# Attention and a wave MLP on one core: q and k of two batches on all 128 partitions, a last key chunk of 128, the last residual by DMA, another order of the steps

## The chip, the core and the metric

The kernel runs on one core of a Trainium2 chip. The core has a matrix engine (PE, with its weight loads listed apart as PEld), three engines for elementwise work (DVE, ACT, POOL) and SP, whose queue issues nearly all DMAs here. Data come from the chip's memory through 16 DMA engines into SBUF, which has 128 partitions; PE writes to PSUM, which has eight banks. The metric is the device time of one execution in microseconds.

## The reference

The inputs are q, k, v of 8 batches, 8 heads, 576 tokens and 64 numbers a head. Two attentions are added, one on tokens averaged in fours, one on a band of three neighbours to each side, and the sum goes through a wave MLP:

```
q_d, k_d, v_d = means of 4 tokens of q, k, v                 # 144 tokens
out_up    = repeat(softmax(q_d k_d^T / 8) v_d, 4 times)      # pooled part
out_local = softmax(q k^T / 8 where |i - j| < 4) v           # band
x     = out_up + out_local, heads side by side               # 8 x 576 x 512
theta = x @ w_theta
y     = w_tok_r @ (x * cos(theta)) + w_tok_i @ (x * sin(theta))   # over tokens
u     = x + y
out   = u + max(u @ w_ch, 0)                                  # float32
```

## The kernel before

Each batch goes through a chain of generator functions; each `next` of one is a step. A string of letters says in which order the steps are taken, and `pin` ties the instructions of every engine to that order, so each engine's queue is in the order of the string. The letters, with the names that the text uses (batch behind the point):

- L `load`, C `cast`: q, k, v from memory in float32 into one of 8 staging buffers, then to bf16. For batches 0 and 1 (`WIDE`) a piece is two heads of q or k, six tokens on each of 96 partitions: pieces q0 to q3 and k0 to k3. From batch 2 on a piece is 2 x 96 tokens of all heads. v has five chunks of keys in three pieces. Casts run on DVE (q), ACT (k) and POOL (v) for batch 0 and on POOL for all others.
- A `turns`: PE turns q and k so that the head's numbers lie on partitions, and pools the tokens. Aq0 to Aq3 and Ak0 to Ak3 in the wide form (`wide_turn`: matmuls into a two-bank buffer, copied by ACT for q, by DVE for k, then DVE sums fours: qdT, kdP), 12 narrower steps else. Avd pools v; POOL multiplies it by `own`.
- S `scores`: Sd0 and Sd1 are the pooled scores, S0 to S4 those of the five chunks of the band; ACT takes exp. Outside the band DVE multiplies by a mask (batch 0), or POOL applies two selects (the others).
- N `pooled_out`: Ng0, Ng1 the pooled output, divided on DVE (xd), Nx its transposes. V `outputs`: V0 to V4 the band's output, divided on DVE (tmp).
- T `transposes`: x transposed, the pooled part added by DVE. H `phases`: theta on PE, sin and cos on ACT (cs). M, Z: x times cos and sin (z).
- X `mix`: X00 to X31, four channel blocks in two halves, 9 matmuls of 288 columns each into psu; DVE adds x (uT). The largest part of the work.
- U `residuals`: for the batches in `DMA_U`, 1 to 6, four DMA transposes of uT into `u_tm`. R `channels`: u @ w_ch into psr. Without the DMA, PE also transposes u (psx) and ACT takes the maximum (rel). O `store`: DVE adds, SP stores.
- l, c, W: the weights' loads (th0, th1, then r, i with their last 64 rows apart, ch), casts, and the nine transposed blocks of the token weights (WT, all needed by X). D: five groups of six warm-up matmuls (wu) on zeros, whose result nobody reads.

Two-bank PSUM buffers (`w2`) come in two copies, one-bank buffers (`w1`) in four; a step that takes a buffer waits until the step that held it has been copied out. The string has a first part, a period of 84 letters that is repeated three times (it takes one batch through every stage), and a last part. X00.0 is the first of the 64 X steps. Around the start the order is

```
Lq0 Lk0 Lq1 Cq0 Ck0 Lk1 Cq1 Aq0 Lq2 Lk2 Ak0 Lq3 Lk3 Ck1 Cq2 Aq1 Lv0 Ak1 Ck2 D0 Lv1 Cq3 Lv2 Aq2 D1 Ak2 Ck3 Aq3 lth0 Ak3 ...
```

all of batch 0, and later `... S3.0 cth0 D2 V0.0 ... Nx.0 V1.0 cr0 S4.0 D3 ... W0 ... T0.0 ... T1.0 ... V2.0 V3.0 H0.0`.

Of the kernel before, what the change touches and what calls it, by code (L numbers as in the profile page):

```python
# [15 lines left out]
P = 128  # L16
B = 8
# [12 lines left out]
KS = [0, 116, 236, 356, 476]  # L30
KW = [128, 128, 128, 128, 100]
# [5 lines left out]
NTR = 6  # L37
TP = TR // 4
# [9 lines left out]
def kernel(  # L48
# [34 lines left out]
    def stage(b, key):  # L83
        t = staged[b, key] = stg.tile([P, 1024], FP32, tag="st", name=f"st{b}_{key}")
        return t

    def load(b):

        if b < WIDE:
            for hh in range(4):  # L90
                for nm, src in zip("qk", (q, k)):
                    nc.sync.dma_start(
                        out=stage(b, f"{nm}{hh}")[0:TR, 0:2 * NTR * D].rearrange("p (h e) -> p h e", h=2),
                        in_=src[b, 2 * hh:2 * hh + 2].rearrange("h (p r) d -> p h (r d)", r=NTR),
                    )
                    yield
        else:
            for nm, src in zip("qk", (q, k)):
                for i in range(3):
                    t = stage(b, f"{nm}{i}")[0:TR].rearrange("p (c h d) -> p c h d", c=2, d=D)  # L100
                    for j in range(2):
                        c = 2 * i + j
                        nc.sync.dma_start(
                            out=t[:, j], in_=src[b, :, TR * c:TR * c + TR, :].rearrange("h p d -> p h d"),
                        )
                    yield
        for i in range(3):
            t = stage(b, f"v{i}").rearrange("p (c h d) -> p c h d", c=2, d=D)
            for c in range(2 * i, min(2 * i + 2, NCH)):
                nc.sync.dma_start(  # L110
                    out=t[0:KW[c], c % 2],
                    in_=v[b, :, KS[c]:KS[c] + KW[c], :].rearrange("h p d -> p h d"),
                )
            yield

    def cast(b):

        q_tm = work.tile([TR, NTR, H, D], BF16, tag="q_tm", bufs=1, name=f"q_tm{b}")
        k_tm = work.tile([TR, NTR, H, D], BF16, tag="k_tm", bufs=1, name=f"k_tm{b}")
# [3 lines left out]
        if b < WIDE:  # L123
            for hh in range(4):
                for i, dst in enumerate((q_tm, k_tm)):
                    eng[i](out=dst[:, :, 2 * hh:2 * hh + 2, :].rearrange("p r h d -> p h r d"),
                           in_=staged.pop((b, f"{'qk'[i]}{hh}"))[0:TR, 0:2 * NTR * D].rearrange(
                               "p (h r d) -> p h r d", h=2, d=D))
# [59 lines left out]
    for lo in (0, 4):  # L188
# [17 lines left out]
    for off in (3, -1):  # L206
# [39 lines left out]
    def weight_casts():  # L246

        for i in range(2):
            act(out=wth[:, 2 * i:2 * i + 2, :].rearrange("p c e -> p (c e)"), in_=staged.pop(("w", f"th{i}")))
# [7 lines left out]
        for i in range(2):  # L257
            gp(out=wch[:, 2 * i:2 * i + 2, :].rearrange("p c e -> p (c e)"), in_=staged.pop(("w", f"ch{i}")))
# [33 lines left out]
    def turns(b):  # L292
# [8 lines left out]
        def wide_turn(n, hh):  # L301
            tm, To = ((q_tm, qT), (k_tm, kT))[n]
            ps = w2(f"pstr{n}{hh}_{b}")
            for r in range(NTR):
                nc.tensor.matmul(
                    out=ps[:, r // 3, (r % 3) * TR:(r % 3) * TR + TR],
                    lhsT=tm[:, r, 2 * hh:2 * hh + 2, :], rhs=ip[:, 0:TR], start=True, stop=True,
                )
            (dve if n == 1 else act)(
                out=To[:, hh, :].rearrange("p (w k c) -> p w k c", k=2, c=3),  # L310
                in_=ps[:, :, 0:3 * TR].rearrange("p k (c w) -> p w k c", w=TR),
# [13 lines left out]
        def turn(n, c):  # L325
            tm, To = ((q_tm, qT), (k_tm, kT))[n]
            ps = w1(f"pstr{n}{c}_{b}")[:, 0:4 * TW].rearrange("p (hh w) -> p hh w", w=TW)
            for hh in range(4):
                nc.tensor.matmul(  # L329
                    out=ps[:, hh, :], lhsT=tm[:, c, 2 * hh:2 * hh + 2, :], rhs=ip, start=True, stop=True,  # L330
# [24 lines left out]
        for c in range(4):  # L355
            nc.tensor.matmul(out=psb[KP * c:KP * c + KP, 0:2 * D], lhsT=PU[1][0:KW[4], :],
# [15 lines left out]
    def scores(b):  # L372
# [43 lines left out]
        for c in range(NCH):  # L416
# [200 lines left out]
    def residuals(b):  # L617

        u = u_tm[b] = moep.tile([P, 4, 4, P], BF16, tag="utm", bufs=1, name=f"utm_{b}")
        for dc in range(4):  # L620
            nc.sync.dma_start_transpose(out=u[:, dc], in_=uTs[b][:, dc, 0:512])
# [45 lines left out]
    def store(b):  # L667
# [20 lines left out]
    DMA_U = (1, 2, 3, 4, 5, 6)  # L688
# [7 lines left out]
        "LLLCCLCALLALLCCALACDLCLADACAlAlCSSSClCSLASlScDVlNCcNAlNlVcSDlLcccWcTCLTcVVLHTAZCLVCHTCWALWWWLLTLLCCA"  # L696
        "LCWZWAAHLLAHWHADLWCSLCCCMZCLLZASlZlLCXSXACANSAACXLCSLNAAAXNSSXVAccCAXTCALVAACVLXLSTTSSHLVVXLTLHCTZRO"
        "AHZZCLHVLROHRLLMCOCSZZCNRLROSLNALOA"
    )
    PERIOD = (  # L700
        "XSCSNTXCCAAXCUAAVAXUACVAXAVAAVXTSSTAXSTAUTHXULCNHZNCAHLZCVHHCZROLLSLMSZRLOZRORLOLROL"
# [3 lines left out]
        "ASXVAAAXAAVXACCNAVXAUTACCCSUTTXTASSCXAHXVZUNHCTHXCAUHZNHZSZLLLRCMOLARORSSCZLRSOOCCNAXAXACAVAAVXXAVTA"  # L705
        "XUSSTARVXSOSXASTTHVUXVTHUNHZUZHNZHRMOSSZRORZORVXSONXTVTXXTVHXVXUHTZXTZHZUUHXZHMURROZROOXXRORXOXXXXRO"
        "ROXRORORORO"
# [61 lines left out]
```

## Time and profile before

| what | value |
|---|---|
| median of 13 runs | 261.26 us (259.7 to 262.89) |
| the profiled execution: time, span | 261.91 us, 260.2 us |
| PE busy (share of the span) | 242.9 us (93%) |
| DVE, ACT, POOL busy | 188.8 (73%), 178.8 (69%), 153.8 (59%) us |
| psu matmuls (L608), 576 of them | 80.0 us busy |
| warm-up matmuls (L282), 30 of them | 12.1 us busy |
| mean granted PE clock | 0.974 |
| DMA moved | 46.73 MB, 180 GB/s on the mean |

Busy times of PE overlap, since its matmuls are pipelined, so that a busy share does not say how many matmuls went through; the counts and the granted clock beside it do. The chain is followed back from the last instruction to what released each step. In the first 40 us PE's count in each 10 us is 26, 60, 85 and 95; from 40 to 50 it is 123.

### The profile page before, as it was taken

How to read it: one execution, taken by the hardware profiler on the slowest of the kernel's cores; microseconds unless marked ns; L12 is line 12 of the kernel's file. 1: busy time of each engine (PE TensorE's matmuls, PEld its weight loads, DVE VectorE, ACT ScalarE, POOL GpSimd, SP SyncE). 2: the span in 40 equal slices, each digit the busy share in tenths (PEclk: the TensorE clock that was granted, in tenths of full speed). 3: DMA queues.
4: the chain of work that ended last, by engine and by line, in shares of the span. 5: the costliest groups of instructions: out<-in, count | busy, mean ns of one | idle time of the engine just before them, and what ended most of it. 6: DMA issues, size and time to landing. Idle time of an engine off the chain costs nothing.

```text
span 260.2 us, 7472 instructions
## 1 busy us (share of the span) xinstructions
PE 242.9 (93%) x2960; PEld 170.1 (65%) x2960; DVE 188.8 (73%) x421; ACT 178.8 (69%) x336; POOL 153.8 (59%) x178
## 2 busy tenths in 40 slices
PE   1769699999999999999999999999999999999993
PEld 1325456678657876588667866687668666776762
DVE  4865869956777787868696868785777588876443
ACT  4349379997889778956896779777886787334022
POOL 4244345579997978398648956797169762600000
PEclk9995679999999999999999999999999999999999
DMA  7999999999999992899689997899399032311324
GB/s 197 231 239 323 260 242 194 214 219 233 220 219 236 237 169 52 195 217 268 126 170 221 279 156 142 177 254 226 58 242 248 23 63 81 105 40 43 142 73 152
DMA packets 120851, 46.73 MB, mean 180 GB/s; under 512 B 110448, under 2 KB 114544, under 8 KB 120816
## 3 DMA queue, kind: packets, MB, share of 16 engines
q1 hardware_dynamic: 120736, 46.18, 80.0%
q8 instruction: 23, 0.38, 0.7%
q14 instruction: 12, 0.10, 0.1%
q10 hardware_dynamic: 80, 0.07, 0.1%
HBM read 33.65 MB, written 9.44 MB: 166 GB/s over the span
## 4 chain that ended last, share of the span: by engine, by line
PE 85%; ACT 5%; DVE 5%; DMA 2%; issue 1%; SPq 0%; DVEq 0%
PE psu L608 27%; PE psr L632 11%; PE psth L546 10%; PE pstr L329 6%; PE psS L421 4%; PE psloc L498 4%; PE wu L282 3%; PE psxt L581 3%; PE xTps L528 3%; DMA st_k<-in_k_dram 2%; PE psnd L460 2%; PE psr L650 2%; PE pstl L557 1%; ACT pm L429 1%; PE psnd L466 1%; PE psxd L483 1%
## 5 line engine op out<-in xcount | busy, mean ns | idle before, releaser
L608 PE MATMUL psu<-WT,z 128*128 128x288 bf16 x576 | 80.0, 286 | 0.0
L608 PEld LDWEIGHTS <-z 128*128 128x128 bf16 x576 | 53.6, 98 | 15.2 <-issue 0.8
L442 POOL TENSOR_SCALAR_AFFINE_SELECT pm<-pm 128x1024 bf16<-128x1024 bf16 (+1 forms) x35 | 36.7, 1047 | 22.2 <-ACT pm L429 22.1
L612 DVE TENSOR_TENSOR uT<-psu,xT 128x288 bf16<-128x288 f32 x64 | 29.2, 456 | 24.2 <-PE psu L608 23.2
L429 ACT ACTIVATE pm<-psS 128x1024 bf16<-128x1024 f32 (+1 forms) x40 | 38.1, 984 | 10.7 <-PE psS L421 10.5
L444 POOL TENSOR_SCALAR_AFFINE_SELECT pm<-pm 128x1024 bf16<-128x1024 bf16 (+1 forms) x35 | 36.7, 1049 | 2.4
L546 PE MATMUL psth<-wth,xT 128*128 128x512 bf16 x128 | 32.9, 379 | 0.4 <-DVE xT L529 0.4
L632 PE MATMUL psr<-wch,uT 128*128 128x512 bf16 x128 | 32.0, 380 | 0.0
L551 ACT ACTIVATE cs<-psth,pihc 128x512 bf16<-128x512 f32 x32 | 22.0, 688 | 11.8 <-PE psth L546 8.0
L529 DVE TENSOR_TENSOR xT<-xTps,xdT 128x480 bf16<-128x480 bf16 (+1 forms) x40 | 24.9, 632 | 5.8 <-PE xTps L528 5.2
L507 DVE TENSOR_TENSOR tmp<-psloc,rl 120x512 bf16<-120x512 f32 (+1 forms) x40 | 27.6, 691 | 1.4
L139 POOL CAST v_w<-st_v 128x1024 bf16<-128x1024 f32 (+1 forms) x24 | 20.8, 896 | 10.6 <-DMA st_v<-in_v_dram 10.6
L582 DVE TENSOR_TENSOR z<-psxt,cs 128x1024 bf16<-128x1024 bf16 x32 | 21.7, 686 | 4.7 <-PE psxt L581 3.1
L133 POOL CAST k_tm<-st_k 96x1024 bf16<-96x1024 f32 x18 | 18.8, 1045 | 9.4 <-DMA st_k<-in_k_dram 8.4
L332 ACT CAST kT<-pstr 128x384 bf16<-128x384 f32 x36 | 18.0, 500 | 7.0 <-PE pstr L329 6.9
L662 ACT ACTIVATE rel<-psr 128x512 f32<-128x512 f32 (+1 forms) x16 | 7.9, 492 | 18.4 <-PE psr L650 15.0
L133 POOL CAST q_tm<-st_q 96x1024 bf16<-96x1024 f32 x18 | 18.4, 1035 | 2.4 <-DMA st_q<-in_q_dram 2.4
L332 ACT CAST qT<-pstr 128x384 bf16<-128x384 f32 x36 | 16.0, 481 | 4.9 <-PE pstr L329 4.7
L552 ACT ACTIVATE cs<-psth 128x512 bf16<-128x512 f32 x32 | 18.9, 590 | 0.0
L673 DVE SCALAR_TENSOR_TENSOR osb<-psr,utm 128x512 f32<-128x512 f32 x24 | 16.3, 687 | 2.3 <-PE psr L632 1.8
L632 PEld LDWEIGHTS <-uT 128*128 128x128 bf16 x128 | 11.1, 98 | 9.8
L498 PE MATMUL psloc<-v_w,pm 128*128 128x65 bf16 (+1 forms) x320 | 17.3, 197 | 0.0
(107 smaller groups left out, 439.1 us busy)
## 6 DMA issues: line engine op xcount, KB each, us to landing
st_v<-in_v_dram SPq DMA_DIRECT2D x32, 256.0 KB, 4.9
out_dram<-osb SPq DMA_DIRECT2D x32, 256.0 KB, 3.6
st_q<-in_q_dram SPq DMA_DIRECT2D x36, 192.0 KB, 4.9
st_k<-in_k_dram SPq DMA_DIRECT2D x36, 192.0 KB, 4.4
st_q<-in_q_dram SPq DMA_DIRECT2D x8, 288.0 KB, 6.1
st_k<-in_k_dram SPq DMA_DIRECT2D x8, 288.0 KB, 12.1
st_v<-in_v_dram SPq DMA_DIRECT2D x8, 200.0 KB
w<-in_moe_w_tok_r_dram SPq DMA_DIRECT2D x2, 576.0 KB
```

The source lines that it names most:

```text
L133: eng[i](out=dst[:, 2 * c:2 * c + 2].rearrange("p c h d -> p (c h d)"), in_=staged.pop((b, f"{'qk'[i]}{c}"))[0:TR])
L332: nc.scalar.copy(out=To[:, :, TR * c:TR * c + TR], in_=ps[:, :, 0:TR])
L429: nc.scalar.activation(out=pv, in_=ps[0:kw].rearrange("p e (j w) -> p (e j) w", w=P)[:, :, 0:qn], func=AF.Exp, scale=SCL,)
L442: nc.gpsimd.affine_select(out=pv, in_=pv, compare_op=ALU.is_ge, fill=0.0, base=off, pattern=[[0, 8], [-1, qn]], channel_multiplier=1)
L444: nc.gpsimd.affine_select(out=pv, in_=pv, compare_op=ALU.is_ge, fill=0.0, base=6 - off, pattern=[[0, 8], [1, qn]], channel_multiplier=-1)
L498: nc.tensor.matmul(out=pv[0:qn, par, j, :], lhsT=pms[b][c][0:kw, 4 * par + j, 0:qn], rhs=v_w[0:kw, c, 2 * j + par, 0:65], start=(j == 0), ...
L507: nc.vector.tensor_tensor(out=tmp[0:cnt].rearrange("p (j e d) -> p e j d", e=2, j=4), in0=pv[0:cnt, :, :, 0:D], in1=rl[0:cnt].unsqueeze(3) ...
L529: nc.vector.tensor_tensor(out=xT[:, :, QS[c]:QS[c] + cnt].rearrange("p e (m j) -> p e m j", j=4), in0=ps[:, :, 0:cnt].rearrange("p e (m j) ...
L546: nc.tensor.matmul(out=th, lhsT=xT[:, dc, P * c:P * c + P], rhs=wth[:, dc, :], start=(dc == 0), stop=(dc == 3),)
L608: nc.tensor.matmul(out=ps[:, 0:288], lhsT=z[:, j, P * dc:P * dc + P], rhs=WT[:, j, cols], start=(j == 0), stop=(j == 8),)
L612: nc.vector.tensor_tensor(out=uT[:, dc, cols], in0=ps[:, 0:288], in1=xT[:, dc, cols], op=ALU.add)
L632: nc.tensor.matmul(out=psr, lhsT=uT[:, dc, P * c:P * c + P], rhs=wch[:, dc, :], start=(dc == 0), stop=(dc == 3),)
```

## The change

- q and k of batches 0 and 1: a piece is now four heads (q0, q1, k0, k1). Heads 4g and 4g + 1 lie on partitions 0 to 63, the next two on 64 to 127, nine tokens of two heads on each partition; each half is a DMA of its own of 288 KB, so there are again 16 such DMAs for the two batches. Two casts for q and two for k take the place of four and four. A turn step has nine matmuls of 64 columns, with half of the identity as the moving operand, where it had six of 96.
- The last chunk of keys has 128 rows (448 to 575) in place of 100. A third pooling matrix (`PU[2]`) and a third mask (`band[2]`) are made for it.
- The last batch joins `DMA_U`: three of its four residual blocks are transposed by DMA, the fourth by PE with a copy on ACT. The maximum and the add of its four large pieces become one DVE instruction each.
- The string of steps is a new one in all three parts; the period is again 84 letters. At the start it now reads (batch 0 where none is given)

```
Lq0 Cq0 Lk0 Aq0 Ck0 Ak0 Lq1 Cq1 Aq1 D0 Ak1 Lk1 Ck1 lth0 Lv0 Aq2 Lv1 Lv2 cth0 Ak2 Cv0 Cv1 Cv2 Aq3 lth1 Ak3 Sd0 lr0 Sd1 lr1 S0 Avd S1 S2 lrt D1 cth1 V0 S3 cr0 cr1 li0 Ng0 li1 crt ci0 Ng1 lit Lq0.1 Lk0.1 Lq1.1 D2 ci1 Lk1.1 cit V1 Cq0.1 Nx V2 W0 T0 ... W1 T1 S4 V3 W2 Cq1.1 W3 ... T2 Lq0.2 Aq0.1 H0 V4 D3 W4 ...
```

  and before X00.0 stand, beside what stood there, S0.1, Ng0.1, Ng1.1, S1.1, Aq0.2 and Aq1.2. The last part ends with `... X21.7 U0.7 U1.7 X30.7 X31.7 U2.7 R4.6 O4.6 U3.7 R0.7 R1.7 O0.7 O1.7 R2.7 O2.7 R3.7 R4.7 O3.7 O4.7`, where it ended with `... X30.7 R4.6 O4.6 R0.7 O0.7 X31.7 R1.7 O1.7 R2.7 O2.7 R3.7 O3.7 R4.7 O4.7`.

```diff
-KS = [0, 116, 236, 356, 476]
-KW = [128, 128, 128, 128, 100]
+KS = [0, 116, 236, 356, 448]
+KW = [128, 128, 128, 128, 128]
 QN = [128, 128, 128, 128, 96]
 NCH = 5
 
 WIDE = 2
 TR = 96
 NTR = 6
+
+WR = 9
+WB = 64
...
-            for hh in range(4):
+            for g in range(2):
                 for nm, src in zip("qk", (q, k)):
-                    nc.sync.dma_start(
-                        out=stage(b, f"{nm}{hh}")[0:TR, 0:2 * NTR * D].rearrange("p (h e) -> p h e", h=2),
-                        in_=src[b, 2 * hh:2 * hh + 2].rearrange("h (p r) d -> p h (r d)", r=NTR),
-                    )
+                    t = stage(b, f"{nm}{g}").rearrange("p (e r d) -> p e (r d)", e=2, d=D)
+                    for i in range(2):
+                        nc.sync.dma_start(
+                            out=t[WB * i:WB * i + WB],
+                            in_=src[b, 4 * g + 2 * i:4 * g + 2 * i + 2].rearrange("h (p r) d -> p h (r d)", r=WR),
+                        )
                     yield
...
+    def wide(t, g):
+
+        return t.rearrange("p c h d -> p (c h d)")[:, 2 * WR * D * g:2 * WR * D * (g + 1)].rearrange(
+            "p (r e d) -> p r e d", e=2, d=D)
+
     def cast(b):
...
-        q_tm = work.tile([TR, NTR, H, D], BF16, tag="q_tm", bufs=1, name=f"q_tm{b}")
-        k_tm = work.tile([TR, NTR, H, D], BF16, tag="k_tm", bufs=1, name=f"k_tm{b}")
+        q_tm = work.tile([P, NTR, H, D], BF16, tag="q_tm", bufs=1, name=f"q_tm{b}")
+        k_tm = work.tile([P, NTR, H, D], BF16, tag="k_tm", bufs=1, name=f"k_tm{b}")
...
-            for hh in range(4):
+            for g in range(2):
                 for i, dst in enumerate((q_tm, k_tm)):
-                    eng[i](out=dst[:, :, 2 * hh:2 * hh + 2, :].rearrange("p r h d -> p h r d"),
-                           in_=staged.pop((b, f"{'qk'[i]}{hh}"))[0:TR, 0:2 * NTR * D].rearrange(
-                               "p (h r d) -> p h r d", h=2, d=D))
+                    eng[i](out=wide(dst, g).rearrange("p r e d -> p e r d"),
+                           in_=staged.pop((b, f"{'qk'[i]}{g}")).rearrange("p (e r d) -> p e r d", e=2, d=D))
                     yield
...
-    for lo in (0, 4):
+    for lo in (0, 4, 32):
...
-    for off in (3, -1):
+    for off in (3, -1, -29):
...
-            for r in range(NTR):
+            flat = ps.rearrange("p k n -> p (k n)")[:, 0:S]
+            for r in range(WR):
                 nc.tensor.matmul(
-                    out=ps[:, r // 3, (r % 3) * TR:(r % 3) * TR + TR],
-                    lhsT=tm[:, r, 2 * hh:2 * hh + 2, :], rhs=ip[:, 0:TR], start=True, stop=True,
+                    out=flat[:, WB * r:WB * r + WB], lhsT=wide(tm, hh // 2)[:, r, :, :],
+                    rhs=ident[:, WB * (hh % 2):WB * (hh % 2) + WB], start=True, stop=True,
                 )
             (dve if n == 1 else act)(
-                out=To[:, hh, :].rearrange("p (w k c) -> p w k c", k=2, c=3),
-                in_=ps[:, :, 0:3 * TR].rearrange("p k (c w) -> p w k c", w=TR),
+                out=To[:, hh, :].rearrange("p (w r) -> p w r", r=WR),
+                in_=flat.rearrange("p (r w) -> p w r", w=WB),
...
-                nc.tensor.matmul(out=psb[KP * c:KP * c + KP, 0:2 * D], lhsT=PU[1][0:KW[4], :],
+                nc.tensor.matmul(out=psb[KP * c:KP * c + KP, 0:2 * D], lhsT=PU[2],
...
-                    in1=band[min(c, 1)][0:kw, 0:qn].unsqueeze(1).to_broadcast([kw, 8, qn]),
+                    in1=band[(0, 1, 1, 1, 2)[c]][0:kw, 0:qn].unsqueeze(1).to_broadcast([kw, 8, qn]),
...
-            nc.sync.dma_start_transpose(out=u[:, dc], in_=uTs[b][:, dc, 0:512])
+            if b < B - 1 or dc < 3:
+                nc.sync.dma_start_transpose(out=u[:, dc], in_=uTs[b][:, dc, 0:512])
+            else:
+                ps = w1(f"psut_{b}", BF16)[:, 0:512].rearrange("p (c t) -> p c t", t=P)
+                for c in range(4):
+                    nc.tensor.transpose(out=ps[:, c, :], in_=uTs[b][:, dc, P * c:P * c + P], identity=ident)
+                nc.scalar.copy(out=u[:, dc], in_=ps)
...
-    DMA_U = (1, 2, 3, 4, 5, 6)
+    DMA_U = (1, 2, 3, 4, 5, 6, 7)
...
-        "LLLCCLCALLALLCCALACDLCLADACAlAlCSSSClCSLASlScDVlNCcNAlNlVcSDlLcccWcTCLTcVVLHTAZCLVCHTCWALWWWLLTLLCCA"
-        "LCWZWAAHLLAHWHADLWCSLCCCMZCLLZASlZlLCXSXACANSAACXLCSLNAAAXNSSXVAccCAXTCALVAACVLXLSTTSSHLVVXLTLHCTZRO"
-        "AHZZCLHVLROHRLLMCOCSZZCNRLROSLNALOA"
+        "LCLACALCADALClLALLcACCCAlASlSlSASSlDcVScclNlccNlLLLDcLcVCNVWTLLCWTSVWCWCLTLAHVDWCTAAHlTZALACHWHCHADA"
+        "ACASZLcWCZSLLSWCMZWLLNZNCAASXAVACCSXALACNSCSLTXAAXVALAXAALVLTlXSCSTHCVLXTLCHVAXTLcAHZZHNHZMCCCLROSCL"
+        "ZNLRRLLOSOLLSZNRROOL"
     )
     PERIOD = (
-        "XSCSNTXCCAAXCUAAVAXUACVAXAVAAVXTSSTAXSTAUTHXULCNHZNCAHLZCVHHCZROLLSLMSZRLOZRORLOLROL"
+        "SSXVCAAXAAUXAACVAXCAVAAUXVAXTCCSSTAXSUTTAHVNXTHZHZNCULCHLCZHRCSOLMSZNRZLRLLLORLOROLO"
     )
     PERIODS = 3
     LAST = (
-        "ASXVAAAXAAVXACCNAVXAUTACCCSUTTXTASSCXAHXVZUNHCTHXCAUHZNHZSZLLLRCMOLARORSSCZLRSOOCCNAXAXACAVAAVXXAVTA"
-        "XUSSTARVXSOSXASTTHVUXVTHUNHZUZHNZHRMOSSZRORZORVXSONXTVTXXTVHXVXUHTZXTZHZUUHXZHMURROZROOXXRORXOXXXXRO"
-        "ROXRORORORO"
+        "AVAASXATASVACLXCAAVVAXAXAVCUSCTCAXAASTAACSXNAACTSTSXULSHVXNCHZVHNTHZTHVUAZUMACHRARCOLOSCZZTLRAOXACVA"
+        "XTSSXVXAZSSTRHONNHZVXHZHSUZVXNMXXUTSSTUZURVROORTHOVXROXVTHXZROTUHXZHHZXXMXZUXURUZROORROXROXOXXXXUUXX"
+        "UROURROORORROO"
     )
```

The rest of the diff gives staging buffers 1152 columns in place of 1024 and takes the part of them that is used.

## Prediction

> **What bounds the kernel now.** I read the page first (the tenths by slice), then the windows, then the chain in order of time, last the timeline where the chain stands still.
>
> ```profile
> span 260.2 us, 7472 instructions
> ...
> PE   1769699999999999999999999999999999999993
> ...
> PEclk9995679999999999999999999999999999999999
> DMA  7999999999999992899689997899399032311324
> ```
>
> PE is full from the seventh slice on, DMA from the second to about 80 us. A full digit does not yet mean work, so I took the distance between back-to-back matmul starts from the trace (psu 122.5 ns, psth and psr 216, psloc 30.5, psS 41, transposes 56, 96-column turns 43, warm-up 216 on the full clock) times the counts: the whole program is 224 us of PE work, 6.5 of it warm-up. PE's last matmul ends at 256.2, so 32 us are lost.
>
> ```profile
> 0.00:10.00 10.00, 2.81 (x26) 2.12 (x27) 6.12 (x40) 4.12 (x5) 4.32 (x19) 1.00 0.85 215
> 20.00:30.00 10.00, 7.66 (x85) 4.20 (x82) 6.96 (x10) 7.08 (x10) 4.85 (x6) 0.67 1.04 318
> 30.00:40.00 10.00, 9.56 (x95) 6.02 (x92) 7.28 (x16) 7.10 (x10) 3.91 (x5) 0.73 1.12 222
> 40.00:50.00 10.00, 9.44 (x123) 6.35 (x123) 9.64 (x20) 9.51 (x19) 5.58 (x7) 1.00 1.05 205
> 60.00:80.00 20.00, 19.86 (x262) 13.80 (x260) 14.50 (x29) 16.61 (x36) 19.73 (x22) 1.00 1.06 221
> 80.00:160.00 80.00, 79.96 (x1059) 58.66 (x1057) 61.43 (x138) 62.38 (x128) 61.02 (x64) 1.00 0.90 188
> ```
>
> Columns: length, then busy time (count) of PE, PEld, DVE, ACT, POOL, clock, DMA share, GB/s. The first 40 us do little work, and their clock falls to 0.67 and 0.73: the clock rows are half speed from 18.25 to 25.08 and from 28.49 to 35.32 us. From 80 to 160 the other engines are at 75 to 80%: PE alone bounds. ACT and DVE are nearly full from 40 to 50, POOL from 60 to 80.
>
> ```profile
> 8.11 0.84 ACT k_tm L126
> ...
> 12.70 2.42 PE wu L282 x6
> ...
> 31.23 2.68 PE wu L282 x6
> ...
> 51.74 1.26 PE psu L608 x9
> ...
> 84.33 1.10 PE psu L608 x9
> ...
> 252.25 0.86 PE psr L632 x4
> ```
>
> The first psu (step X00.0) starts at 51.74 with 25.5 us of PE work before it in the order: 26.2 of the 32 us are lost there. Batch 1's X00.1 starts at 84.33 with 55.8: another 2.3. The remaining 172 us lose 3.8. So two things can be won: the start, and PE work itself.
>
> **The change, part by part**, against the profiled run: 260.2 span, 261.91 with what lies around it, 0.65 above the median of 261.26.
>
> Last residual (b = 7). PE loses 16 transposes (L642) and gains 4: 12 x 56 ns = -0.67. PE has no gap to 256.2, so it counts whole. ACT loses four rel of 0.60 and gains one copy of about 0.6; DVE's adds stay near 0.69 each. SP gets three DMA transposes (2.4 us to landing). U0 and U1 stand behind X21.7, U2 behind X31.7, but it needs only X20 and X21; its landing is about 1 us after X31.7 ends. The PE part U3.7 needs X31.7's add (0.46), covered by R4.6 (0.67). The first add O0.7 waits for all four parts, 1.9 us after X31.7, when psr0 is ready. The end stays R4.7, rel, add, store. Bounds: -0.9 (the rel queue goes too) and +0.5 (a transpose lands 1.2 us late and the four one-bank buffers fill). I take -0.67.
>
> Wide turns. 144 matmuls of 64 columns for 96 of 96: 9 x 29 ns (pstl's 64-column row: 16 in 0.47 us) against 6 x 43: nothing, at most 16 x 9 x 1.5 ns = +0.2. Evacuations and sums keep their sizes.
>
> Casts of q, k. The row for 128x1152 is wtm: 1.15 on ACT, 1.14 on POOL. ACT 2 x 1.15 for 4 x 0.83 (-1.0), POOL 4 x 1.14 for 8 x 0.82 (-2.0), DVE 2 x 0.80 at most for 4 x 0.535 (-0.5). All wait for loads, so what counts is the last one's latency: +0.3. Two more constants cost POOL about 1.6 and DVE 0.25; POOL's first cast is at 15.30, DVE's first q cast moves from 4.67 to 5.0, when its second DMA lands.
>
> Last key chunk of 128. Same columns on PE, same free sizes on ACT and POOL; 8 x 56 KB more to load, against 185 GB/s some 0.3 us of DMA per batch, prefetched; below nothing too, since the 4-byte completion packets (3680 = 177 x 16 + 8 x 10 + 24 x 32) suggest that 100 rows ran on 10 of the 16 DMA engines. Zero.
>
> Loads of q, k in batches 0, 1: 2304-byte packets to 64 partitions for 1536-byte packets to 96, as many bytes. The old ones took 105 ns, 96 for each DMA engine a batch: 10.1 us. 2304-byte packets took 93 to 100 ns to 128 partitions (21 to 25 us), 160 on average about the first 64-partition token-weight load (25.0 to 26.4), 198 about the second (29.1 to 31). 64 x 100 = 6.4; 64 x 198 = 12.7. The second load of each pair goes to the other half, so that DMA engines that drift apart spread; I take 157 ns, the old time, and keep -3.7 and +2.6 a batch.
> The Trainium skill (page "SBUF — State Buffer", Door 1: The DMA port swizzle) speaks against this change: partitions 0 to 63 reach 8 of the 16 ports, so that a 64-row transfer has half the rate, about 218 GB/s; the rows of 160 and 198 ns agree. By it eight loads of 288 KB take 10.8 us, +0.7 a batch, and the sum below would be about -0.9, an estimate.
>
> The new start, at the old rate of loads. (1) The last k of batch 0 lands at 13.2 as before; cast 1.15, turn 0.4, then on DVE 0.75 + 0.65 + 0.24 + 0.74 + 0.75 + 0.65 + 0.24: Sd1.0 at 18.8 (before 19.08). (2) Before, two warm-ups stood in the way of the turns and D3 in front of W0 and T0:
>
> ```profile
> 31.16 2.74 PE L282 MATMUL wu<-warm,ident 128*128 128x512 bf16 x6
> ...
> 34.93 0.82 POOL L126 CAST k_tm<-st_k 96x768 bf16<-96x768 f32 x1 [5.96 <-DMA st_k<-in_k_dram]
> 35.05 1.22 DVE L529 TENSOR_TENSOR xT<-xTps,xdT 128x480 bf16<-128x480 bf16 x2 [2.37 <-PE xTps L528]
> ```
>
> DVE waited 2.37 us for the transposes behind D3. Now D2 is between Ng1.0 and V1.0, where PE waits for DVE's xd anyhow, and D3 behind H0.0. T1.0's add would end near 34.6, not 36.27. But Aq0.1 now stands ahead of H0.0 on PE, and q0.1 is loaded behind all token weights: 7776 KB come before its end, and before the change 7720 KB had landed at 34.8. So 35.0, + cast 1.14: H0.0 at 36.5 (before 36.33), with 12.8 us of work done (13.0). Behind the waiting Aq0.1 on PE are H0, V4, D3; ACT's next too. What was stalled by D3 is now stalled by q0.1: +0.4. (3) H0.0 to X00.0 took 15.41 us for 12.46 of work. Now there are 14.8 of work, among it D3 and D4 and, new ahead of X00.0, S0.1, Ng0.1, Ng1.1, S1.1 and two turns. ACT must do 17.8 us of rows until W8 is copied, but its rows overlap (cs starts 1.06 apart for two, WT copies 0.6): 15.4. Both give about 51.9. Lost before X00.0: 51.9 - 27.6 = 24.3 against 26.2. Against it, PE waits for q0.1 from about 33.5, and a half-clock stretch of 3.4 us after it costs 1.7; I count half a one. Start: -1.9 + 0.85, about -1.1. Bounds -4 (loads at 100 ns, T1's 34.6 then decides) and +3.
>
> X00.0 to the period: POOL is the cover. Batch 1's selects (2 x 1.05 each) stand among casts of batch 2 from about 48 on; V0.1 comes 8 us earlier than before and V3.1, V4.1 meet their selects within 0.3 us. 0, from -0.5 to +1.5.
>
> Period and last part: the same work on each engine. Counting PE work between steps of the new order: a two-bank buffer is wanted again at the earliest 0.40 us after its evacuation would be over (S3 to V0; before 0.70), one-bank buffers 0.41 (0.41), a select 5.5 us ahead of its V (2.9). No wait comes up that repeats three times. U3 to R0 is shorter, 1.5 us of work, but SP issues it as soon as X31's add is done, 5 us before R0. 0, from -1 to +1.
>
> Sum: -0.67 - 1.1 = -1.8 on 261.91, 260.1; on the median 259.4.
>
> **Rivals.** Loads slow (other side): mean packet near 190 ns. Batch 0's last k lands 2 us late, q0.1 2.5 us late, H0.0 at 39, and everything behind it: 259.4 + 2.5 + some POOL, 262 to 264. For it: the 160 and 198 rows; against: alternate halves, and that 1536-byte packets, two thirds of them to the same half, took 65 ns while few were in flight. It decides from 180 ns up (80 packets until q0.1 x 23 ns = 1.8).
> Loads fast: 100 to 120 ns; q0.1 lands 3 us sooner, H0.0 at 34.6: 256.5 to 258.5. For it: the 93 ns rows.
> Gain eaten: a whole cold window (+1.7) in place of the half, or POOL's selects late (+1.5): 260.3 to 262.2. For it: POOL's 19.73 of 20, D1 no longer in the turns to raise the clock; against: D2 and the work around it fill 28 to 31.
>
> **How the numbers follow.** Forecast (258.5 to 260.4) 0.42, loads fast 0.20, gain eaten 0.24, loads slow 0.14. 0.3% (0.8 us) is about what a measurement tells. Faster: forecast and fast, 0.60; within: 0.12; slower: 0.28. Range: 256.6 to 262.6, leaving out the far ends of fast and slow.
>
> **What would show it.** Right: eight q, k loads down by 13 us; Sd1.0's scores near 18.8; PE idle on POOL's q_tm before H0 near 36; first psu near 52 with S1.1 ahead of it; periods of 27.4 us as before; from the last psu to the last psr 4 us of PE without a gap and no rel but the last. Wrong: packets of q, k far from 157 ns; half-clock rows past 36; PE waits on POOL's pm between 54 and 74; a period longer than 27.6.

## The result, and the profile after

The changed kernel took 264.2 us at the median (263.04 to 265.2, 11 runs) against 260.78 for the kernel before on the same chip (258.55 to 263.05, 48 runs): a ratio of 1.014, interval 1.0116 to 1.0164. It is 1.4% slower, where I had said 259.4 us and 6 chances in 10 for faster, and outside my range of 256.6 to 262.6. The profiled execution took 264.42 us with a span of 262.7 (before: 261.91 and 260.2), so it lost 2.5 of the 3.4 us. Here and below a median is that of all runs, while ratios and classes by clock leave out the slow runs, those more than 1.5% over the fastest of their kernel: 12 of the 131 runs of the kernel before beside the experiments, none of the changed kernel, three of new_order_kact (263.4 us without them) and at most one of any other.

From the page of the changed kernel, the span and three rows of tenths by slice:

```profile
span 262.7 us, 7535 instructions
...
PE   0548699899999999999999999999999999999993
...
PEclk9986979959999999999999999999999999999999
DMA  6999998999999998999859996999818132422535
```

PE is full from the seventh slice on, as before, but the ninth slice is new: a clock of 0.5 in the middle of full work. The windows of the changed kernel (length, busy time and count of PE, PEld, DVE, ACT, POOL, then clock, DMA share, GB/s) put a number to it; the last line is the kernel before from 50 to 60:

```profile
0.00:10.00 10.00, 0.78 (x12) 0.63 (x13) 4.28 (x36) 3.07 (x3) 5.14 (x24) 1.00 0.79 179
20.00:30.00 10.00, 8.50 (x107) 4.98 (x108) 6.21 (x12) 6.94 (x9) 6.63 (x7) 0.78 1.06 342
30.00:40.00 10.00, 7.77 (x88) 5.05 (x85) 7.31 (x14) 7.73 (x12) 2.29 (x2) 0.83 1.07 227
40.00:50.00 10.00, 9.76 (x147) 6.56 (x145) 9.00 (x17) 8.92 (x17) 4.99 (x5) 1.00 0.97 198
50.00:60.00 10.00, 9.16 (x109) 6.50 (x106) 6.97 (x14) 6.78 (x11) 8.39 (x9) 0.66 1.01 197
...
80.00:160.00 80.00, 80.00 (x1060) 58.77 (x1059) 59.35 (x134) 62.84 (x128) 61.74 (x65) 1.00 0.99 200
...
50.00:60.00 10.00, 9.98 (x144) 7.47 (x143) 6.38 (x17) 9.54 (x17) 7.55 (x9) 1.00 1.04 227
```

Three things to see: in the first 10 us PE does 12 matmuls in place of 26, and the DMAs move 179 GB/s in place of 215; from 50 to 60 the clock is 0.66 in place of 1.00; from 80 to 160 PE's row is that of before. The clock rows of the trace are half speed from 17.51 to 24.34, 34.58 to 37.99 and 51.64 to 58.47 us, all multiples of 3.41 us long.

The chain of waits of the changed kernel, in order of time (start, duration, what):

```profile
8.67 1.16 ACT k_tm L136
11.02 2.56 PE wu L291 x6
...
57.98 1.46 PE psu L618 x9
...
87.46 1.21 PE psu L618 x9
```

In what follows, X00.0 and its like are the start of a step's first matmul: X00.0 at 57.91 (before 51.74), X00.1 at 87.39 (before 84.17), the last psr matmul done at 258.39 (before 256.07). So the loss is made ahead of X00.1, 3.2 us, and 0.9 come back behind it: X00.1 to the last psr takes 171.0 us against 171.9.

Where PE stands on the way shows in the timeline of the changed kernel, taken engine by engine (start, duration, engine, what; in brackets the idle time of that engine before it and what ended it):

```profile
31.89 1.15 ACT L262 CAST wtm<-w 128x1152 bf16<-128x1152 f32 x1 [1.68 <-DMA w<-in_moe_w_tok_i_dram]
...
33.10 0.29 PE L278 MATMUL wps<-ident,wtm 128*128 128x128 bf16 x2 [1.94 <-ACT wtm L262]
...
35.13 1.15 POOL L136 CAST q_tm<-st_q 128x1152 bf16<-128x1152 f32 x1 [5.85 <-DMA st_q<-in_q_dram]
...
37.00 1.51 PE L556 MATMUL psth<-wth,xT 128*128 128x512 bf16 x4
...
42.82 1.15 POOL L136 CAST k_tm<-st_k 128x1152 bf16<-128x1152 f32 x1 [1.45 <-DMA st_k<-in_k_dram]
...
50.36 0.24 DVE L332 TENSOR_REDUCE kdP<-kT 128x24 bf16<-128x96 bf16 x1
...
50.51 0.24 PE L393 MATMUL psSd<-qdT,kdP 64*128 64x144 bf16 x2 [0.35 <-DVE kdP L329]
...
51.47 0.49 PE L431 MATMUL psS<-qT,kT 64*128 64x128 bf16 x8 [0.49 <-ACT pd L403]
...
57.37 0.61 PE L431 MATMUL psS<-qT,kT 64*128 64x128 bf16 x8
...
57.91 1.53 PE L618 MATMUL psu<-WT,z 128*128 128x288 bf16 x9
```

W1 waits 1.94 us for the token weights w_i, H0.0 starts at 37.00 (before 36.33), the last sum of batch 1 (kdP) is done at 50.61, and from there to X00.0 another 7.3 us go by, most of them on half the clock.

### The profile page after: what moved, and what is told of

Its sections match the earlier page's. It is cut to its first block, busy times and chain, and to the rows that moved or that the text cites. A ratio compares the mean times of both kernels' runs of the same rounds, so it can differ in the third digit from the quotient of the medians.

```text
span 262.7 us, 7535 instructions
## 1 busy us (share of the span) xinstructions
PE 240.8 (92%) x2996; PEld 170.7 (65%) x2996; DVE 187.8 (71%) x421; ACT 176.3 (67%) x331; POOL 153.8 (59%) x179
## 4 chain that ended last, share of the span: by engine, by line
PE 86%; DMA 6%; ACT 2%; SPq 2%; DVE 2%; issue 0%; ACTq 0%
PE psu L618 28%; PE psth L556 11%; PE psr L648 11%; PE pstr L339 6%; DMA w<-in_moe_w_tok_i_dram 4%; PE psS L431 4%; PE psloc L508 4%; PE xTps L538 4%; PE psxt L591 3%; DMA st_k<-in_k_dram 2%; PE wu L291 2%; PE psnd L470 2%; PE psr L666 2%; PE pstr L315 2%; PE pstl L567 1%; PE wps L278 1%
## 5 line engine op out<-in xcount | busy, mean ns | idle before, releaser
L648 PE MATMUL psr<-wch,uT 128*128 128x512 bf16 x128 | 31.4, 379 | 0.0
L148 POOL CAST v_w<-st_v 128x1024 bf16<-128x1024 f32 (+1 forms) x24 | 21.1, 896 | 13.6 <-DMA st_v<-in_v_dram 12.0
L689 DVE SCALAR_TENSOR_TENSOR osb<-psr,utm 128x512 f32<-128x512 f32 x28 | 19.0, 689 | 6.3 <-PE psr L648 4.6
L678 ACT ACTIVATE rel<-psr 128x256 f32<-128x256 f32 (+1 forms) x12 | 5.4, 456 | 24.2 <-PE psr L666 23.9
L648 PEld LDWEIGHTS <-uT 128*128 128x128 bf16 x128 | 11.3, 98 | 10.4
```

The source lines that it names most:

```text
L648: nc.tensor.matmul(out=psr, lhsT=uT[:, dc, P * c:P * c + P], rhs=wch[:, dc, :], start=(dc == 0), stop=(dc == 3),)
```

## The experiments

Two theories at the start. **Loads**: two halves of 64 partitions load slowly, and everything that waits for q and k is late. **Order**: the new order loses time by itself, whatever the loads do. A third, **clock**, is that the half-clock rows cost the time. Each run below stands against the kernel before, timed beside it on the same chip (medians of 260.5 to 261.6 us).

### The loads, in both orders

The old order with the new loads. The edit is `load`, `cast`, `wide` and `wide_turn` of the change in the kernel before, and in the string every second L and C of q and k in batches 0 and 1 left out, since a piece is now twice as large:

```
- Lq0 Lk0 Lq1 Cq0 Ck0 Lk1 Cq1 Aq0 Lq2 Lk2 Ak0 Lq3 Lk3 Ck1 Cq2 ...
+ Lq0 Lk0 Cq0 Ck0 Aq0 Lq1 Lk1 Ak0 Cq1 ...
```

> The order, the residual and the key chunk of before; only q, k of batches 0 and 1 are loaded, cast and turned as in the change (two halves of 64 partitions, 2304-byte packets). Theory loads (64 partitions load at 165 ns a packet, 0.6 us a batch slower and every later load with it): batch 0's last k lands near 13.7, q0.1 and what follows 0.5 to 1.5 us later than before, +1 to +2 us: ratio 1.004 to 1.008. Theory order (W1 and the turns in front of X00.0 starve PE, whatever the loads do): within 0.5 us of before, ratio 0.998 to 1.002, first psu near 51.7. Theory clock (the half-clock stretch at 51.6 to 58.5 is what cost the time): as the order theory, unless a half-clock row begins after 50 us.

Measured: 266.5 us, ratio 1.0226 (1.0175 to 1.0277), far more than the 1 to 2 us that the loads theory had given.

The same with 128 partitions. Slot e of partition half i holds head 4g+2e+i, so that one DMA fills all partitions, and the readers of heads look up where a head lies:

```
-   for i in range(2):
-       out=t[WB * i:WB * i + WB],
-       in_=src[b, 4*g + 2*i:4*g + 2*i + 2].rearrange("h (p r) d -> p h (r d)", r=WR)
+   for e in range(2):
+       out=t[:, e],
+       in_=src[b, 4*g + 2*e:4*g + 2*e + 2].rearrange("h (p r) d -> (h p) (r d)", r=WR)
+   def place(b, h):
+       return (2 * (h // 4) + h % 2, h % 4 // 2) if b < WIDE else (h // 2, h % 2)
```

> The same, but each load fills all 128 partitions (slot e of partition half i holds head 4g+2e+i, and the readers of the heads are renamed to match); order, residual and key chunk of before. Theory loads: packets near 100 ns, batch 0's last k lands near 10, q0.1 to k1.1 3 to 7 us earlier than before, and the time is 0.5 to 2 us under before (0.992 to 0.998). Theory order: loads are not what PE waits for, ratio 0.998 to 1.002. Against old_order_64 the loads theory says at least 2 us less.

Measured: 261.7 us, ratio 1.0032 (1.0004 to 1.0060). The 4.8 us between the two are the loads' (the packets and the bytes are the same), but I had expected this one to be faster than before. Its timeline shows one reason; the last line is the kernel before:

```profile
7.09 1.28 ACT L140 ACT_TABLE_LOAD   x1 [7.09 <-DMA st_k<-in_k_dram]
8.38 1.15 ACT L140 CAST k_tm<-st_k 128x1152 bf16<-128x1152 f32 x1
...
0.80 1.28 ACT L126 ACT_TABLE_LOAD   x1 [0.80 <-PEq L753]
```

ACT's table load stands behind the wait for the first k. The cast of k is ACT's first instruction here, but that alone is not the reason: so it is in the kernel before, where the table load ran at 0.80. There the cast waits for one DMA and here for two; whether that decides it was not tried. Two more runs take that away, with a copy of one column at the start:

```
+   early = const.tile([P, 1], FP32, name="early")
+   nc.scalar.copy(out=early, in_=pihc)
```

> old_order_64 with a one-column copy on ScalarE at the very start, so that its table load (1.28 us) does not stand behind the wait for the first k load, as it did there at 8.44 and in old_order_128 at 7.09 us. If that load was on the path: about 1.3 us less than old_order_64, 265.2, ratio 1.016; if not, 266.5 again, 1.022. Either way the loads theory keeps old_order_64_t well above 1.005.

> old_order_128 with the same early copy. If the table load was on the path: 260.4, ratio 0.998, and 64 partitions against 128 stay 4.5 us apart; if not, 261.7. The order theory (the new order is itself worth 2 us or more once the loads are fast) says that it stays more than 1.5 us above new_order_128's 258.4; if it comes down to 259 or less, the order is worth nothing.

Measured: 266.8 us, ratio 1.0207 (1.0170 to 1.0243), and 260.1, ratio 0.9980 (0.9950 to 1.0010). With 128 partitions the table load was on the path (1.6 us). With 64 the medians show no gain: the cast of k began at 9.18 in place of 9.74, since the load landed at 9.18 in one profiled run and at 8.44 in the other. The loads' share in the old order is then 6.7 us. PE's waits in old_order_64_t (what waits, for what, us in total, times, longest) show where it sits:

```profile
PE pstr L317 <- DVE q_tm L136: 6.9, 1, 6.9
PE pstr L317 <- POOL k_tm L136: 4.7, 1, 4.7
```

The second row is Ak0.1, which the old order puts far ahead: it waits 4.7 us for k0.1. In old_order_128_t that wait is gone, and the first row is 5.4. H0.0 to the last sum of batch 1 takes 19.5 us in old_order_64_t and 13.6 in old_order_128_t.

The new order with 128 partitions (the change with the edit above):

> The changed kernel with all its parts and its order, only with 128-partition loads. Theory loads: q0.1 lands near 31 instead of 35, k1.1 near 36 instead of 42.7, w_i near 28.5; W1 does not wait, first psu at 52 to 54 instead of 57.9, and at least 2 of the 2.8 to 3.4 us come back: 259.5 to 262, ratio 0.993 to 1.003. Theory order: PE is starved at 48 to 52 by ACT's and DVE's rows and not by loads: 263 or more, ratio 1.008 to 1.014, first psu past 56. Theory clock: first psu sooner, but a half-clock stretch somewhere ahead of it, 262 to 263.5.

Measured: 258.4 us, ratio 0.9884 (0.9831 to 0.9937): faster than the kernel before, 5.8 us under the change, and better than any of the three theories had it. From its timeline, beside the rows of the change above:

```profile
29.63 1.15 POOL L140 CAST q_tm<-st_q 128x1152 bf16<-128x1152 f32 x1 [3.27 <-PE psloc L514]
...
34.21 1.15 POOL L140 CAST k_tm<-st_k 128x1152 bf16<-128x1152 f32 x1 [0.46 <-DMA st_k<-in_k_dram]
...
53.50 1.28 PE L624 MATMUL psu<-WT,z 128*128 128x288 bf16 x9
```

q0.1 is cast at 29.6 (35.1), k1.1 at 34.2 (42.8), H0.0 starts at 33.40 (37.00), X00.1 at 82.73 (87.39). The DMA records give the reason: a 2304-byte packet of batch 0 took 163 ns on the mean into 64 partitions and 107 into 128 (157 to 163 and 106 to 112 in the other runs of either kind); with 64 packets for each of 16 DMA engines that is 10.4 us against 6.9.

The new order with the loads and turns of before (two 96-partition pieces to a step, cast together):

```
-   t = stage(b, f"{nm}{g}").rearrange("p (e r d) -> p e (r d)", e=2, d=D)
+   t = stage(b, f"{nm}{g}")[0:TR].rearrange("p (h e) -> p h e", h=4)
-       out=t[WB * i:WB * i + WB], in_=... r=WR
+       out=t[:, 2 * i:2 * i + 2], in_=... r=NTR
```

> The changed kernel with its order, residual and key chunk, but q, k of batches 0 and 1 loaded and turned as before the change (96 partitions, 1536-byte packets, two old pieces to a step, cast together; warm-up reads 256 zeros twice). The old packets took 105 ns, 10.1 us a batch, against 10.5 for the 64-partition halves. Theory halves (the 64-partition layout is the loss): the first psu before 55, X00.1 before 85, time 260 to 261.5, ratio to before 0.996 to 1.003. Theory order (the order needs loads faster than either of these two; with loads at the old rate it loses): X00.1 at 85.5 to 87, time 262.5 to 264, ratio 1.006 to 1.013.

Measured: 262.7 us, ratio 1.0065 (1.0031 to 1.0099): within what the order theory had given for the time. Its profiled run, the fastest of the twelve (260.75 us), had X00.1 at 83.71, which was the other theory's figure. The old 1536-byte packets took 100 ns here, 9.6 us for batch 0, q0.1 was cast at 33.2. So the 64 partitions cost 1.5 us against the loads of before, and the order with the small parts, which was to win 1.8 us, loses 1.7 at these loads.

128 partitions for batch 0 alone:

```
+   if b == 0: nc.sync.dma_start(out=t[:, e], in_=heads.rearrange("h (p r) d -> (h p) (r d)", r=WR))
+   else:      nc.sync.dma_start(out=t[WB * e:WB * e + WB], in_=heads.rearrange("h (p r) d -> p h (r d)", r=WR))
```

> The changed kernel with 128-partition loads for batch 0 alone; batch 1 keeps the 64-partition halves. Theory queue (one load queue, so 4 us saved in batch 0 move every later load, and the early wait of W1 for w_i goes): most of new_order_128's gain, 259 to 261.5, ratio to before 0.993 to 1.002, q0.1 near 31.5, q1.1 to k1.1 still 2.55 us apart. Theory spacing (batch 1's turns are bunched because its own halves come 2.55 us apart): under half of the gain, 261.5 to 264.

Measured: 261.2 us, ratio 0.9989 (0.9955 to 1.0024). Batch 0 gives 3.0 of the 5.8 us, batch 1 the other 2.8 (by the ratios 1.5 and 1.1 of 2.6%); neither theory takes most of it. The medians together (us):

| loads of q, k, batches 0 and 1 | 96 partitions | 64 | 128 |
|---|---|---|---|
| order of before | 260.8 | 266.5, early table load 266.8 | 261.7, early table load 260.1 |
| new order, residual, key chunk | 262.7 | 264.2 | 258.4 |

So the new order with the small parts has no fixed price. By the ratios, each against the kernel before on its own chip, the second row is 0.65% slower than the first with 96 partitions, but 0.7 to 0.9% faster with 64 and 1.0 to 1.5% with 128.

### From H0.0 to the first psu

ACT copies batch 1's four turned k in place of DVE, with 64 and with 128 partitions:

```
-   (dve if n == 1 else act)(
+   (dve if n == 1 and b == 0 else act)(
```

> The changed kernel, 64-partition loads, but ScalarE copies batch 1's four turned k out of PSUM in place of VectorE (4 x 0.75 us). Theory VectorE (from T3.0's add at 40.9 to the last kdP sum at 50.5 VectorE has 9.7 us of rows without a gap, and PE waits for the end of it): Sd1.1 1.5 to 3 us sooner, 261 to 262.7, ratio to before 1.001 to 1.007. Theory ScalarE (it is as full there: 8.9 of 10 us): Sd1.1 within 0.5 us of 50.5, time 263.5 to 264.7, ratio 1.010 to 1.015.

> new_order_128 with batch 1's four k copies on ScalarE in place of VectorE. In new_order_kact it won nothing, 264.0, where k1.1 landed at 42.8; here the loads are 7 us early and VectorE has 12.6 us of rows without a gap (37.6 to 50.2). Theory VectorE: Sd1.1 at 45 to 46 in place of 47.25 and 1 to 2 us less than new_order_128, 256.5 to 257.5, ratio 0.982 to 0.987. Theory both full (ScalarE has 9.5 of 10 us there): within 0.7 us of 258.4.

Measured: 264.0 us, ratio 1.0087 (1.0052 to 1.0121), and 259.6, ratio 0.9934 (0.9897 to 0.9972), 1.2 us more than new_order_128. DVE alone is not the bound: with 3 us moved off it, Sd1.1 came 13.9 us behind H0.0 in new_order_kact and 13.3 in new_order_128_kact (45.98 against 32.67), as in the change, new_order_128, new_order_128_b0 and new_order_96 (13.2 to 13.9). ACT takes its place: it is busy 8.92 of 10 us from 40 to 50 in the change, and in new_order_128_kact 9.96 of the 10 us from 36 to 46, where DVE is at 6.68.

W1 to W3 and Aq0.1 moved from in front of H0.0 to behind it, with 64 partitions, and with 128 together with the move of D4 below:

```
- W1 T1.0 S4.0 V3.0 W2 Cq1.1 W3 Ck1.1 Lv2.1 T2.0 Lq0.2 Aq0.1 H0.0 V4.0 D3 W4
+ T1.0 S4.0 V3.0 Cq1.1 Ck1.1 Lv2.1 T2.0 Lq0.2 H0.0 W1 V4.0 W2 Aq0.1 D3 W3 W4
```

> The changed kernel, 64-partition loads, with W1, W2, W3 and Aq0.1 moved from in front of H0.0 to behind it (W1, V4.0, W2, Aq0.1, D3, W3). Theory waits: T1.0 comes near 31.2 in place of 33.8 and H0.0 at 33 to 34.5 in place of 37.0; k1.1, cast at 44, then holds Ak2.1, so 1 to 1.6 us are won: 262.4 to 263.3, ratio to before 1.005 to 1.009. Theory loads alone (batch 1's turns wait for their loads whatever stands before them): 263.7 to 264.7, ratio 1.010 to 1.014.

> new_order_128_d4 with the same move of W1 to W3 and Aq0.1. With 128-partition loads PE waits only 0.3 to 0.6 us there, so the theory of waits says -0.5 to 0 against 257.9: 257.4 to 258, ratio 0.984 to 0.988. If VectorE's rows behind Aq0.1 set the first psu, the later Aq0.1 costs 0.3 to 1 us: 258.2 to 259.

Measured: 265.0 us, ratio 1.0112 (1.0072 to 1.0152), by the ratio what loads alone had given, and 258.4, ratio 0.9885 (0.9838 to 0.9933), no gain either. In new_order_w H0.0 came at 33.09 as wanted and the last sum at 48.30, yet Sd1.1 at 51.33, later than the change's 50.51. PE's longest wait from 30 to 60 us in new_order_w:

```profile
PE psva L363 <- POOL v_w L148: 2.1, 1, 2.1
```

That is Avd.1, which waits for batch 1's v, cast when its load lands. The 1.94 us that PE stands for w_i in the change was not had back by this move: PE came to the next late load sooner and waited there, and behind that wait the clock rows of this trace are at half speed from 48.49 to 58.73, three pieces in place of the change's two.

What sets the first psu can be read from the traces (it was not tried by an edit of its own). From H0.0 to the last kdP sum of batch 1 it takes 13.6 us in the kernel before, 13.6 in the change, 13.3 in new_order_96 and new_order_128_b0. What differs is what follows. In the timeline of the kernel before:

```profile
49.67 0.24 DVE L322 TENSOR_REDUCE kdP<-kT 128x24 bf16<-128x96 bf16 x1
...
49.78 0.64 ACT L274 COPY WT<-wps 128x576 bf16<-128x576 bf16 x1
...
50.44 1.28 ACT L393 ACT_TABLE_LOAD   x1
...
50.91 0.24 PE L383 MATMUL psSd<-qdT,kdP 64*128 64x144 bf16 x2
...
51.74 1.26 PE L608 MATMUL psu<-WT,z 128*128 128x288 bf16 x9
```

X00.0 starts 1.8 us behind the last sum (49.91); W8 is copied before ACT loads its table for exp. In the timeline of new_order_128_b0, a run without a half-clock row there:

```profile
46.55 0.24 DVE L337 TENSOR_REDUCE kdP<-kT 128x24 bf16<-128x96 bf16 x1
...
46.69 0.23 PE L398 MATMUL psSd<-qdT,kdP 64*128 64x144 bf16 x2 [0.23 <-DVE kdP L334]
...
47.78 0.40 PE L436 MATMUL psS<-qT,kT 64*128 64x128 bf16 x8 [0.61 <-ACT pd L408]
...
48.90 0.56 PE L283 MATMUL wps<-ident,wtm 128*64 128x128 bf16 x10
...
51.41 0.40 PE L436 MATMUL psS<-qT,kT 64*128 64x128 bf16 x8
...
51.74 1.28 PE L625 MATMUL psu<-WT,z 128*128 128x288 bf16 x9
```

Here 4.9 us lie between the sum (46.79) and X00.0: S0.1, W7, W8, Ng0.1, Z4.0, Ng1.1, two turns and S1.1 are all behind Sd1.1. Five more traces of the new order without a half-clock row there have 4.8 (the two with the copies on ACT 5.8), and all eight of the old order 1.8 to 2.4. The change has 7.3; the 2.4 us more fall on its half-clock rows.

What stands ahead of X00.0 need not be done behind it. From the last sum to X00.1 it takes 34.3 to 35.8 us in the old order and 34.0 to 35.7 in those eight traces of the new one: the moved steps cost nothing on balance, and won nothing. In the change it takes 36.8.

### The clock

D4 moved from in front of Aq3.1 to behind Z2.0, where PE waits for DVE anyhow, in three kernels (64, 128 and 96 partitions):

```
- Ak2.1 D4 Aq3.1 Ak3.1 Cq0.2 Avd.1 Sd0.1 Z1.0 Lq2.2 cch0 W6 Cq1.2 Z2.0 Sd1.1
+ Ak2.1 Aq3.1 Ak3.1 Cq0.2 Avd.1 Sd0.1 Z1.0 Lq2.2 cch0 W6 Cq1.2 Z2.0 D4 Sd1.1
```

> The changed kernel, 64-partition loads, only warm-up D4 moved from in front of Aq3.1 to behind Z2.0, where PE waits for VectorE's last sum of batch 1 (1.3 us of matmuls in place of idle time). Theory clock (PE idles at 48 to 51.5, so the clock is halved at 51.6 and that costs 2 to 3 us before the first psu): no half-clock row after 48 us in most runs, mean clock 0.975 to 0.985 where the change had 0.966 to 0.980, 262 to 263, ratio 1.004 to 1.008. Theory loads alone: the clock row costs little, 263.7 to 264.7, ratio 1.010 to 1.014.

> new_order_128 with the same move of D4. Theory clock: 0.5 to 1.5 us under new_order_128's 258.4, 257 to 258, ratio 0.985 to 0.989. Theory loads alone: 258 to 259.

> new_order_96 (new order, loads of before) with D4 behind Z2.0. Theory clock (the order's loss is the half-clock rows that PE's idle time before Sd1.1 brings on): mean clock 0.98 or more in most runs, 260.8 to 261.8, ratio to before 0.999 to 1.003. Theory waits (W1 and Aq0.1 in front of H0.0): 262.2 to 263, ratio 1.004 to 1.008.

Measured: 263.3 us, ratio 1.0079 (1.0048 to 1.0109); 257.9, ratio 0.9862 (0.9819 to 0.9906), the lowest ratio of all; 262.8, ratio 1.0050 (1.0014 to 1.0086), no change. The windows of new_order_d4 at the place:

```profile
50.00:60.00 10.00, 9.75 (x137) 6.80 (x136) 8.86 (x19) 8.91 (x14) 8.45 (x10) 1.00 1.26 197
```

The clock is 1.00 in place of 0.66. With 64 partitions the move gave 0.9 us by the medians (0.6% by the ratios), and the median of the mean clocks went from 0.968 to 0.979. With 128 partitions all six runs had 0.983 or more, but the 0.5 us won lie within the two intervals. With 96 the trace still has a half-clock row ahead of X00.0 (49.85 to 53.27). How little work brings the half clock is not shown: in the 3.41 us ahead of the row at 51.64 of the change PE was busy 2.36 us, and from 46.24 to 49.65 in new_order_d4, with no such row behind, 2.08. The clock differs from run to run of one kernel, so I put the runs in classes by the mean clock granted (mean us, number of runs):

| mean clock | before | change | new_order_96 | new_order_d4 |
|---|---|---|---|---|
| 0.960 to 0.970 | none | 264.6 (6) | 264.0 (3) | 262.8 (1) |
| 0.971 to 0.981 | 261.6 (40) | 263.8 (5) | 262.8 (6) | 263.2 (11) |
| 0.982 to 0.988 | 260.7 (65) | none | 261.3 (3) | none |
| 0.989 and over | 260.0 (14) | none | none | none |

At the same clock the change loses 2.2 us, by the one class that both have. The other 1.2 of its 3.4 go with lower clocks: the kernel before had 0.982 or more in 79 of 119 runs, the change in none. In the first three columns a class lower goes with 0.7 to 1.5 us more. By the same classes new_order_96 loses 0.6 to 1.2 of its 1.7 us. The table can't tell a time that is longer for its clock from a clock that is lower for PE's waits.

### The small parts

Residual and key chunk on the kernel before, together and each alone, with the tail from X20.7 on in the changed kernel's order where the residual needs it:

```
- KS = [0, 116, 236, 356, 476]; KW = [..., 100]; DMA_U = (1, 2, 3, 4, 5, 6)
+ KS = [0, 116, 236, 356, 448]; KW = [..., 128]; DMA_U = (1, 2, 3, 4, 5, 6, 7)
```

> The kernel before with only the last residual by DMA (its tail in the changed kernel's order from X20.7 on) and the last key chunk of 128 rows. All theories agree here: the 12 transposes fewer take 0.67 us off PE, the wider chunk nothing: ratio to before 0.9974 (0.996 to 0.999), and from the last psu group to the last psr group no gap on PE. If it is 1.000 or more, one of the two parts that I costed at -0.67 and 0 is a loss, and has its share in the 3 us that the whole change lost.

> The kernel before with only the last residual mostly by DMA (tail in the changed kernel's order from X20.7 on). If the term -0.67 stands alone: 260.2 to 260.5, ratio 0.9965 to 0.9985. If the gain is lost by itself: 0.999 to 1.001.

> The kernel before with only the last key chunk of 128 rows. My term was 0: ratio 0.9985 to 1.0015. If the chunk costs what the residual wins: +0.5 to +0.8 us, ratio 1.002 to 1.003, and the loss lies ahead of 80 us (more bytes on a full load queue, two more constants on POOL).

Measured ratios: 0.9997 (0.9963 to 1.0031), 1.0003 (0.9971 to 1.0035), 1.0037 (0.9998 to 1.0076). The intervals are wider than the terms. In the traces X00.1 to the last psr takes 171.9 us before, 171.2 in residual_only, 171.1 in small_parts, 171.7 in chunk_only: the residual's 0.7 is there. In the three upper clock classes, of two to five runs each, residual_only is 0.4 to 0.8 us under the kernel before and chunk_only 0.2 to 0.4 over it.

The old key chunk in new_order_128_d4 (`KS`, `KW` and the constants as before):

> new_order_128_d4 with the old last key chunk of 100 rows. If the chunk costs 0.5 to 0.8 us: 257.1 to 257.4, ratio to before 0.983 to 0.986; if it costs nothing: 257.6 to 258.2, 0.986 to 0.988.

Measured: 257.3 us, 0.6 under new_order_128_d4, ratio 0.9891 (0.9860 to 0.9922) against its own runs of before. The runs of the kernel before that stand beside the two differ by 0.5 themselves, so the medians speak for a gain and the ratios against one. Whether the chunk costs 0.3 to 0.5 us or nothing stays open.

## Why the prediction was wrong, by its own steps

**Last residual, -0.67:** right by the traces. X00.1 to the last psr takes 0.7 us less in residual_only and, with all parts, 0.9 in the change; the end grew by 0.2, from 4.1 to 4.3 us behind the last psr. The medians are too wide to show it.

**Wide turns and casts:** no run showed a cost that would need another term. **Last key chunk, 0:** not refuted, more likely +0.3.

**Loads, 157 ns a packet, "the old time":** the packet was nearly right, "the old time" was not. The packets took 163 ns in batch 0 (157 to 163 in the six kernels with these loads), and the old ones 97 where I had taken 105, the mean of both batches. So batch 0 takes 10.4 us against 9.3 and not the same. My 93 to 100 ns for 128 partitions was low too: the mean of the 2304-byte packets from 21 to 25 us is 110. q0.1 landed at 35.0 as I had said, but the same order with the old loads casts it 2.0 us sooner (33.2): my 35.0 came from bytes landed in the old order. That is 1.5 us of the time. The Trainium skill (page "SBUF — State Buffer", Door 1: The DMA port swizzle), which I had set against my term, had the direction right: it gives a 64-row transfer half the rate, about 218 GB/s, and here 163 ns a packet on 16 DMA engines is 226 GB/s. Half it was not: into 128 partitions 107 ns is 344 GB/s, 1.52 times as much.

**The new start, -1.1, is the step that failed.** Sd1.0 came at 19.95 (18.8), W1 stood for w_i, which I had not seen among the waits, and H0.0 came at 37.0 (36.5). All this is 0.5 us at H0.0. The failure is step (3): "ACT must do 17.8 us of rows until W8 is copied, but its rows overlap ...: 15.4. Both give about 51.9." I took the larger of PE's 14.8 and ACT's 15.4 and let the rest run beside. But 15.4 was the old order's 13.6 to the last sum and 1.8 behind it, and the new order puts 4.9 behind it, in a row: 18.5, 3.1 more. The runs new_order_96 and new_order_128_b0, without a half-clock row there, take 18.1 and 18.2 from H0.0 to X00.0. The work that I had put into the waits came behind the last of them, and the waits stayed. I had counted 0.85 for half a half-clock stretch behind the wait for q0.1; one is there (34.58 to 37.99; its price is within the 0.5 at H0.0), and a second, of twice its length, cost 2.4 ahead of X00.0. 0.5, 3.1 and 1.55 make the 5.2 us between my 52.75 (51.9 and 0.85) and 57.91.

**X00.0 to the period, 0:** 1.0 us came back. X00.0 to X00.1 takes 29.5 us for 28.2 of work, so 1.3 are lost there where I had carried over 2.3. X00.1 is late by 4.1 against my steps, and the time by 4.3 (264.42 for 260.1).

**Period, 0:** right; 27.25 us, for 27.36 before.

**Rivals.** Loads slow was to give 262 to 264 and did, nearly, but by other means: its packets were to reach 180 ns and stayed at 163, and it needed no more, since the cold clock and the row of steps behind Sd1.1 were added. Loads fast (256.5 to 258.5 at 100 to 120 ns) is new_order_128: 107 ns, 258.4 us. Gain eaten had a whole cold window in place of the half: it is there, but the dear one is the second, longer one. My chances were wrong in holding these apart: slow loads and low clocks came together (0.978 to 0.986 in old_order_64, 0.984 to 0.992 in old_order_128). That PE's waits for late loads bring the half clock is likely from new_order_d4, and not shown.

## What to carry to other kernels

Count the partitions that a DMA writes before its packet size: here the same bytes in the same packets went about 1.5 times as fast into 128 partitions as into 64, and a renaming of heads that adds no instruction turned a loss of 1.4% into a gain of 1.2%, 1.4% with one warm-up moved.
When steps are pulled in front of a milestone, ask of each which result it waits for: what stands behind the last late result adds up in a row, and a maximum over engines does not see it.
An order is worth what the loads under it allow: the same one, with the small parts, lost 0.65% with 96 partitions and won at least 1.0% with 128.
A stretch where PE waits a little, again and again, may be paid twice, by the wait and by the clock behind it. A warm-up group moved to where PE waits gave 0.9 us in one kernel, 0.5 within the noise in a second and nothing in a third, so it has to be measured.

## What the runs showed of the hardware

- Half-clock rows come in pieces of 3.41 us, at another phase in each run (the first begins at 18.25 us in the kernel before, 17.51 in the change, 14.97 in new_order_128 and 17.35 in new_order_96), and one kernel's runs spread with it: new_order_96 took 260.75 us at a mean clock of 0.987 and 264.31 at 0.967. The Trainium skill (page "TensorE: Matmul & The Clock Gate", Part 1: The HAM clock gate (the "warmup" mystery)) tells of a free-running window of 3413 ns; the rows agree.
- A row's price depends on what PE has to do in it: the two rows from 51.64 to 58.47 fell on full work and went with 2.4 us more ahead of X00.0, while those before 40 us fell partly among waits.
- ACT's table load (1.28 us) stood behind the DMA wait of ACT's first instruction in old_order_128 and old_order_64 (7.09 and 8.44 us) and ran at 0.80 in the kernel before and in the change; with fast loads an early one-column copy won 1.6 us.
- The product zl on DVE, the same form each time, took 0.41 to 0.43 us in the kernel before where POOL stood still and 0.69 to 0.91 where POOL worked beside it; in the change one beside POOL took 1.50, but three others 0.41 to 0.42. So POOL at work is not enough to slow it. What more it takes was not tried.
